# Attention and a state-space layer in one Trainium2 kernel: which score tiles go to VectorE, when a score fill is issued, and who goes first

## The chip, the cores and the metric

The kernel runs on one core of a Trainium2 chip. The core has five engines that matter here: TensorE (matrix products, "PE"), ScalarE (activation functions, "ACT"), VectorE ("DVE"), GpSimd ("POOL") and SyncE ("SP", which issues most DMA transfers). Each engine has its own in-order instruction stream and they meet through semaphores. Matrix products go to PSUM, which has eight banks of 512 float32 columns in each of 128 partitions. The metric is device time in microseconds; a comparison uses the median of several executions.

## What is computed

Two independent layers run on their own inputs, and their outputs are joined along the last axis.

```
# A: a diagonal complex state-space layer, L = 2048 steps, 640 states and channels
Lam_bar = exp(dt * Lam);  B_bar = ((Lam_bar - 1) / Lam)[:, None] * Bmat
h[t] = Lam_bar * h[t-1] + x[t] @ B_bar.T
y = 2 * Re(hseq @ Cmat.T) + x * Dskip
# B: attention, 2048 rows, 32 query heads of 20 channels, one key and one value head
q = x @ wq;  k = x @ wk;  v = x @ wv
p = softmax(q k^T * 20**-0.5)          # per head, no mask
out = concat_heads(p @ v) @ wo
```

The attention has 32 x 2048 x 2048 scores, each of which needs an exponential. That is by far the largest elementwise work of the kernel.

## The kernel before

**Tiles.** Heads are taken four at a time: eight head groups, for each of four blocks of 512 query rows. The code numbers these 32 blocks `b` (called head groups below). A block has 64 score tiles: 16 blocks of 128 keys times the four heads `j` of the group. A tile is 128 keys x 512 queries, fills one PSUM bank, and is one matmul of 32 contracted rows (20 channels, and one row that carries a bound for the softmax). Four tiles with four different `j` can run side by side in the array, since each uses its own 32 rows. There are 2048 tiles in all (`NTILE`).

**Two ways to an exponential.** Five banks belong to ScalarE: slot `SC0` of three banks and slot `SC1` of two. TensorE fills a slot (`fill`), ScalarE turns it into bf16 probabilities in one of seven buffers `PR` (L1040), and meanwhile the other slot is filled. About a fifth of the tiles go to VectorE instead: they are written to one of two other banks (`MB0`, `MB1`, which all other tasks share), and VectorE makes a first pass over the bank, an add and a clamp with int16 output whose bits are a coarse bf16 power (`fill_d`, into one of 18 buffers `DR`). Three shifted copies of that buffer (`copy`, by `copy_source` on VectorE or `pool_source` on GpSimd, one or two tiles at a time) make up the other terms of the approximation. So a VectorE tile has four entries in the product with V, a ScalarE tile one.

**PV.** The products with V accumulate a whole head group in the bank `MB2` (`pv_source`, `pv`). A group of four such matmuls, one for each head `j`, runs side by side in four column quarters. The `PR` or `DR` buffer that a matmul reads is free again when it is done. At the end of a head group VectorE evacuates the bank (`pvsb`, L1257) and the sums go through DRAM to be inverted and spread, so that the output can be normalized (`normalize`).

**Everything else** is cut into tasks with a due time in tiles, which `manager` starts when one of the two shared banks is free: projections of the queries, rows of the softmax bound, the state-space layer's input products (`unit_task`) and outputs (`y_task`), and the output projection (`o_task`). The state-space scans and their products run on VectorE.

**The order is planned when the program is built.** `Schedule` plays the engines with an assumed duration for each step (`dur`), and writes each engine's instructions in the order in which that play starts them. On the chip the order is fixed, and semaphores hold an engine until what it needs is there. An engine takes the ready step with the lowest `prio`. A step of `prio` at most `URGENT` (1.0) that will be ready soon holds back any step whose own `prio` is above 1.0 and which would run into it; steps at or below 1.0 are not held. A score fill has `prio` 0; `TASK`, `PV`, `ALONE` (a VectorE tile on its own) are TensorE's other priorities; `EV` (evacuations), `P1` (first pass), `COPY` and `COPY1` (copies), `CLOSE` (copies at the end of a group) are VectorE's. `port` marks steps of VectorE and GpSimd that must not overlap in the plan. `hurry` marks late state-space steps, which then get a priority of about 0.46, but only `PAUSE` ns after the last such step. `OVERDUE` is the number of tiles by which a task may be late before only the most urgent tasks are started.

**Which tile goes where.** Before, tiles are numbered in one sequence (`tile_n`). A fill takes the next three or two for ScalarE, and up to the fourth place of the array goes to VectorE if a shared bank and `DR` buffers are free (`want_d`) and VectorE's share stays below a quarter (`SHARE`); of the numbers taken, the one whose `j` has gone to VectorE least often is given to it (`d_weight`). The fill is issued as soon as its slot is free.

Of the kernel before, what the change touches and what calls it, by code (L numbers as in the profile page):

```python
# [9 lines left out]
ALU = mybir.AluOpType  # L10
# [10 lines left out]
class Op:  # L21


    __slots__ = ("eng", "fns", "dur", "deps", "prio", "reads", "writes", "prev", "gate", "hook", "start", "end",
                 "seq", "land", "dma_key", "idx", "tail", "mode", "load", "late", "port", "after")

    def __init__(self, eng, fns, dur, deps=(), prio=5, reads=(), writes=(), prev=None, gate=None, hook=None,
                 dma_key=None, land=0.0, tail=0.0, mode="F", load=0.0, port=False):
        self.eng, self.fns, self.dur = eng, list(fns), dur
        self.deps, self.prio, self.prev = list(deps), prio, prev  # L30
        self.reads, self.writes = list(reads), list(writes)
        self.gate, self.hook = gate, hook
        self.dma_key, self.land, self.tail = dma_key, land, tail
        self.mode, self.load, self.late = mode, load, False
        self.port, self.after = port, []
        self.start = self.end = None
        self.seq = self.idx = 0


class Schedule:  # L40
# [12 lines left out]

    PAUSE = 3300.0
    LOCK = 60.0
# [95 lines left out]
    def pick(self, eng):  # L151
        urgent = None
        t = self.t
        cands = self.pending[eng]
        for src in self.sources[eng]:
            extra = src()
            if extra is not None:
                cands = cands + [extra]
        can, held = [], []
        for op in cands:  # L160
            r = self.ready(op)
            if r is None:
                continue
            if op.gate is not None and not op.gate():
                continue
            if r <= t + 1e-6:
# [230 lines left out]
class Build:  # L397
# [189 lines left out]
    def program(self):  # L587
        self.tile_n = 0
        self.free_banks = list(self.banks)
        self.qt_op, self.row_op = {}, {}  # L590
# [388 lines left out]
    def attention(self):  # L979
# [10 lines left out]
        while self.tile_n < NTILE:  # L990
# [5 lines left out]
            n = min(self.CHUNKS[i], NTILE - self.tile_n)  # L996
            b0, b1 = self.tile_n // 64, min(self.tile_n + n, NTILE - 1) // 64
            yield lambda: self.block_ready(b0) and self.block_ready(b1)
            deps = list(self.slot_last[i])
            for b in sorted({b0, b1}):  # L1000
                deps += [self.row_op[self.row_key(b)]]
            deps += [self.kt_op[tb] for tb in range(4)]
            if k == 0:
                deps += self.tabs
            fill = self.pe([], self.mmt(512, 2), deps=deps, prio=0, mode="S", hook=lambda op, i=i: self.fill(op, i))
            k += 1

        for i in (k % 2, (k + 1) % 2):
            yield lambda: fill.start is not None and all(o.start is not None for o in self.slot_last[i])
            for bank in self.slots[i][1]:  # L1010
                bank.last, bank.busy = list(self.slot_last[i]), False
                self.misc.append(bank)
                self.free_banks.append(bank)

    def fill(self, op, i):
        p = self
# [3 lines left out]
        self.nhold += 1  # L1020
        tiles = list(range(self.tile_n, self.tile_n + n))
        self.tile_n += n
        extra = []
        while len(tiles) < 4 - len(extra) and self.want_d(len(extra)):
            tiles.append(self.tile_n)
            self.tile_n += 1
            extra.append(min(tiles, key=self.d_weight))
            tiles.remove(extra[-1])
            self.d_per[extra[-1] // 64, extra[-1] % 4] += 1
        ents = []  # L1030
# [3 lines left out]
        for m in extra:  # L1034
# [5 lines left out]
        ex = self.act(lambda e: e.activation(dst, t[:, 0:512 * n], ACT.Exp, scale=1.0 / UNIT),  # L1040
                      0.8333 * 512 * n + 50,
                      deps=[op], reads=[b.key for b in banks[:n]], writes=[f"PR{h.index}"], prio=0.5,
# [22 lines left out]

    def d_weight(self, m):

        return self.d_per[m // 64, m % 4], m

# [8 lines left out]
    def d_source(self):  # L1078

        if not self.started or not self.d_count or not self.want_d():  # L1080
            return None
        b = self.tile_n // 64
        if not self.block_ready(b) or self.d_per[b, self.tile_n % 4] > min(self.d_per[b, j] for j in range(4)):
            return None
        row = self.row_op[self.row_key(b)]
        if row.end is None or self.s.seen(row, "pe") > self.s.t:
            return None

        def hook(op):
            self.d_per[self.tile_n // 64, self.tile_n % 4] += 1  # L1090
            self.tile_n += 1
            self.fill_d(op, self.tile_n - 1)
            op.reads = sorted(set(op.reads))
        return Op("pe", [], self.mmt(512), prio=self.ALONE, mode="S", load=128.0, hook=hook)

    ALONE, TASK, PV = 1.9, 1.6, 2.0
    EV, P1, COPY, COPY1 = 0.52, 0.5, 0.49, 0.6
    CLOSE, PVEV = 0.3, 0.3
# [15 lines left out]
    def fill_d(self, op, m):  # L1114
# [9 lines left out]
        key = f"DR{h.index}"  # L1124
        first = self.dve(self.ts(p.DR[:, h.index, :], bank.ap, 16256.0, 0.0, ALU.add, ALU.max), 605, deps=[op],
                         reads=[bank.key], writes=[key], prio=self.P1)
# [13 lines left out]
    def copy_source(self):  # L1140
# [10 lines left out]
        k = can[0][2][0]  # L1151
        two = [d for d in can if k in d[2]][:2 if n >= 2 else 1]
        one = len(two) == 1
        if one and any(d[1].end is None or d not in can for d in self.d_open):
# [3 lines left out]
        if can[0][3] == self.pv_b and self.pv_filled[self.pv_b] == 64:  # L1158
            prio = self.CLOSE
        return Op("dve", [], 200 if one else 333, prio=prio, port=True, hook=lambda op: self.copy(op, k, two))  # L1160

    BACKLOG = 9

    def pool_source(self):
# [6 lines left out]
        two = [d for d in can if k in d[2]][:2]  # L1171
        if len(two) < 2:
            return None
# [543 lines left out]
    in_use = 0  # L1717
    OVERDUE = 120

# [75 lines left out]
```

## Time and profile before

| | us |
|---|---|
| median of 9 runs | 780.97 |
| lowest and highest | 779.97 and 782.89 |
| the profiled execution | 779.97 |
| its span in the profile | 777.9 |
| ScalarE busy | 757.5 |
| TensorE busy (matmul records) | 728.6 |
| VectorE busy | 656.8 |
| GpSimd busy | 379.7 |

The profile is one execution, recorded instruction by instruction. Busy time is the union of an engine's instructions. A line such as "L1040 ACT ACTIVATE PR<-SC ... x655 | 740.7, 1432 | 1.9 <-PE MB L569 1.5" is a group of equal instructions: the line of the code, engine, operation, what it writes and reads, how many there are, their busy time in us and the mean duration of one in ns, and then how long the engine was idle just before them and what released it. "MB" are the shared banks and the PV bank, "SC" the two slots of ScalarE. The chain of work is followed back from the last instruction: at each step to whatever released it. In its rows the first number is a start and the second a duration, both in us. TensorE's 32-row and 32-column matmuls are quarters of the array, so four of them lie beside each other in time.

### The profile page before, as it was taken

How to read it: one execution, taken by the hardware profiler on the slowest of the kernel's cores; microseconds unless marked ns; L12 is line 12 of the kernel's file. 1: busy time of each engine (PE TensorE's matmuls, PEld its weight loads, DVE VectorE, ACT ScalarE, POOL GpSimd, SP SyncE). 2: the span in 40 equal slices, each digit the busy share in tenths (PEclk: the TensorE clock that was granted, in tenths of full speed). 3: DMA queues.
4: the chain of work that ended last, by engine and by line, in shares of the span. 5: the costliest groups of instructions: out<-in, count | busy, mean ns of one | idle time of the engine just before them, and what ended most of it. 6: DMA issues, size and time to landing. Idle time of an engine off the chain costs nothing.

```text
span 777.9 us, 23546 instructions
## 1 busy us (share of the span) xinstructions
PE 728.6 (94%) x10148; PEld 236.5 (30%) x10150; DVE 656.8 (84%) x1249; ACT 757.5 (97%) x680; POOL 379.7 (49%) x395
## 2 busy tenths in 40 slices
PE   8999998899889999999998999999999999999898
PEld 3322222222223232223222323223222322333224
DVE  5988999999998978799998878788989878757994
ACT  5999999999999999999999999999999999999995
POOL 7044455555444112645546563464453565567552
PEclk9999999999999999999999999999999999999999
DMA  9830200000000000020000000010000010010001
GB/s 209 131 82 10 51 9 10 9 3 10 8 9 23 23 17 17 23 43 12 15 16 9 24 22 21 24 37 17 10 15 16 4 29 22 23 31 20 11 7 38
DMA packets 54183, 21.55 MB, mean 28 GB/s; under 512 B 43464, under 2 KB 54080, under 8 KB 54080
## 3 DMA queue, kind: packets, MB, share of 16 engines
q1 hardware_dynamic: 52072, 19.87, 11.4%
q8 instruction: 80, 1.31, 0.7%
q10 hardware_dynamic: 2008, 0.18, 0.2%
q14 instruction: 23, 0.19, 0.1%
HBM read 7.20 MB, written 5.50 MB: 16 GB/s over the span
## 4 chain that ended last, share of the span: by engine, by line
ACT 82%; PE 14%; DVE 2%; DMA 1%; issue 0%; ACTq 0%; DVEq 0%
ACT PR L1040 82%; PE MB L569 5%; PE SC L569 5%; PE MB L565 4%; DVE DR L584 1%; PE SC L565 1%; DMA vrow<-in_A_Dskip_dram 1%; DVE WO L716 0%; DVE xbT L793 0%; ACTq L550 0%; DVE fr L584 0%; DVE pvsb L1257 0%; DVE g L1553 0%; DVE wq L781 0%; DVE aq L583 0%
## 5 line engine op out<-in xcount | busy, mean ns | idle before, releaser
L1040 ACT ACTIVATE PR<-SC 128x1536 bf16<-128x1536 f32 (+1 forms) x655 | 740.7, 1432 | 1.9 <-PE MB L569 1.5
L579 POOL TENSOR_TENSOR DR<-DR,step 128x512 int32<-128x512 int32 x356 | 365.8, 1049 | 380.1 <-DVE DR L584 160.2
L584 DVE TENSOR_SCALAR DR<-MB 128x512 int16<-128x512 f32 x412 | 273.9, 683 | 75.1 <-PE MB L569 71.7
L569 PE MATMUL SC<-QT,KT 32*128 32x512 bf16 x1636 | 255.3, 383 | 38.7 <-ACT PR L1040 27.6
L569 PE MATMUL MB<-DR,VS 128*32 128x512 bf16 x1648 | 226.9, 384 | 2.6 <-DVE pvsb L1257 1.3
L569 PE MATMUL MB<-PR,VP 128*32 128x512 bf16 x1636 | 227.0, 385 | 1.0 <-DVE pvsb L1257 0.9
L569 PEld LDWEIGHTS SC<-QT,KT 32*128 32x128 bf16 x1636 | 66.2, 90 | 288.8 <-ACT PR L1040 220.5
L569 PE MATMUL MB<-QT,KT 32*128 32x512 bf16 x412 | 151.0, 384 | 0.7 <-DVE DR L584 0.6
L584 DVE TENSOR_SCALAR DR<-DR 128x1024 int16<-128x1024 int16 (+1 forms) x289 | 105.1, 416 | 4.0 <-PE MB L569 3.2
L569 PEld LDWEIGHTS MB<-PR,VP 128*32 128x32 bf16 x1636 | 56.8, 94 | 66.3 <-issue 48.5
L569 PEld LDWEIGHTS MB<-DR,VS 128*32 128x32 bf16 x1648 | 56.2, 94 | 66.0 <-issue 35.4
L565 PE MATMUL MB<-xaT,BT 128*32 128x512 bf16 x800 | 62.3, 382 | 0.0
L579 DVE TENSOR_TENSOR prod<-MB,Z 128x1024 bf16<-128x1024 f32 x40 | 48.6, 1215 | 6.8 <-PE MB L565 6.2
L569 PE MATMUL MB<-xbT,wqf 128*32 128x512 bf16 x640 | 47.8, 382 | 0.3 <-DVE brow L584 0.3
L565 PE MATMUL MB<-WO,OT 128*32 128x128 bf16 (+1 forms) x928 | 41.5, 292 | 0.0
L569 PEld LDWEIGHTS MB<-QT,KT 32*128 32x128 bf16 x412 | 35.4, 91 | 18.6 <-DVE DR L584 8.6
L1553 DVE TENSOR_TENSOR_SCAN g<-sc,hst,u 128x512 bf16<-128x512 f32 x30 | 38.9, 1299 | 0.0
L565 PE MATMUL MB<-CT,W 128*32 128x512 bf16 (+1 forms) x640 | 31.3, 301 | 0.0
L565 PE MATMUL MB<-CT,xbT 128*32 128x512 bf16 (+1 forms) x640 | 30.1, 301 | 0.0
L579 DVE TENSOR_TENSOR prod<-g,tab 128x1024 bf16<-128x1024 bf16 x40 | 29.3, 733 | 0.0
L1376 DVE CAST stg<-MB 128x512 bf16<-128x512 f32 x35 | 23.8, 681 | 6.3 <-PE MB L565 6.0
L569 PE MATMUL MB<-KT,VZ 128*32 128x256 bf16 x504 | 28.5, 275 | 0.0
(124 smaller groups left out, 377.1 us busy)
## 6 DMA issues: line engine op xcount, KB each, us to landing
out_dram<-stg SPq DMA_DIRECT2D x35, 128.0 KB, 1.7
rdB<-recs SPq DMA_DIRECT2D x124, 32.0 KB, 1.8
CT<-in_B_x_dram SPq DMA_DIRECT2D x2, 640.0 KB, 5.5
WO<-in_B_wo_dram SPq DMA_DIRECT2D x4, 200.0 KB
wqf<-in_B_wq_dram SPq DMA_DIRECT2D x1, 680.0 KB, 5.9
out_dram<-PR SPq DMA_DIRECT2D x5, 128.0 KB, 1.9
sums<-pvsb SPq DMA_DIRECT2D x31, 4.0 KB
dn<-sums SPq DMA_DIRECT2D x31, 4.0 KB, 1.9
```

The lines of the kernel that those rows point to most:

```text
L565: r = e.matmul(out[32 * j:32 * j + 32], lhsT=lhsT[:, 32 * j:32 * j + 32], rhs=rhs, start=start, stop=stop, tile_position=(0, 32 * j), skip ...
L569: return lambda e: e.matmul(out, lhsT=lhsT, rhs=rhs, start=start, stop=stop, **kw)
L579: return lambda e: e.tensor_tensor(out, a, b, op)
L584: return lambda e: e.tensor_scalar(out, a, s1, s2, op0=op0, op1=op1)
L1040: ex = self.act(lambda e: e.activation(dst, t[:, 0:512 * n], ACT.Exp, scale=1.0 / UNIT), 0.8333 * 512 * n + 50, deps=[op], reads=[b.key fo ...
L1376: ev = self.dve(lambda e: e.tensor_copy(st, bank.ap), 620, deps=[prev], reads=[bank.key], writes=[key], prio=self.EV, gate=(lambda: last.e ...
L1553: o = self.dve(lambda e, ri=ri, init=init: e.tensor_tensor_scan(p.g[:, u, ri, :], rdec, p.u[:, ri, :], init, ALU.mult, ALU.add), 1280, por ...
```

## The change

The list of tiles becomes, for each head group and head `j`, a queue of key blocks (`rem`). ScalarE takes its tiles from the head group at hand, and of it from the head with most tiles left (`take_tile`); VectorE takes tiles from that group while more than 10 tiles (`AHEAD`) are left in it, and else from the next group (`d_block`, `take_d`), if that group's queries are there and enough `DR` buffers remain for the copies that are still owed (`can_d`, `due_copies`). A copy takes one tile instead of two when the second belongs to a later group and buffers are short (`short`). A fill has a gate (`fill_now`): while the other slot's exponential runs, and no shared bank is free but one will be, the fill waits for the bank, at most until 650 ns (`MARGIN`) before that exponential ends, so that it can take a VectorE tile along. A gated fill counts as urgent from that moment (`due`). Copies come after first passes and evacuations (`COPY` 0.49 to 0.56), tasks of TensorE come before PV and are no longer held for a fill (`TASK` 1.6 to 0.95), `OVERDUE` goes from 120 to 400 and `PAUSE` from 3300 to 1000. The planner's assumed durations are changed for the exponential, the first pass and VectorE's copies.

```diff
-    PAUSE = 3300.0
+    PAUSE = 1000.0
@@ Schedule.pick
             if op.gate is not None and not op.gate():
+                if op.due is not None and r <= t + 1e-6 and (urgent is None or op.due < urgent):
+                    urgent = op.due
                 continue
@@ attention
-            b0, b1 = self.tile_n // 64, min(self.tile_n + n, NTILE - 1) // 64
-            yield lambda: self.block_ready(b0) and self.block_ready(b1)
+            near = [self.act_block()]
+            if self.remaining(near[0]) < n + 2 and near[0] + 1 < NQB * NGG:
+                near.append(near[0] + 1)
+            yield lambda: all(self.block_ready(b) for b in near)
...
             fill = self.pe([], self.mmt(512, 2), deps=deps, prio=0, mode="S", hook=lambda op, i=i: self.fill(op, i))
+            fill.gate = lambda op=fill, i=i, n=n: self.fill_now(op, i, n)
+    MARGIN = 650.0
+    def fill_now(self, op, i, n):
+        s = self.s
+        other = self.slot_last[1 - i]
+        if len(other) != 1 or other[0].start is None or not self.d_count:
+            return True
+        op.due = other[0].start + other[0].dur - self.MARGIN
+        if s.t >= op.due or not self.can_d() or len(self.d_free()) < len(self.SHIFTS):
+            return True
+        if len(self.d_banks()) >= self.WANT:
+            return True
+        for b in self.free_banks:
+            if all(o.end is not None for o in b.last):
+                r = max(s.seen(o, "pe") for o in b.last)
+                if s.t < r <= op.due:
+                    s.at(r)
+                    return False
+        return True
+    WANT = 1
@@ fill
-        tiles = list(range(self.tile_n, self.tile_n + n))
-        self.tile_n += n
-        extra = []
-        while len(tiles) < 4 - len(extra) and self.want_d(len(extra)):
-            tiles.append(self.tile_n)
-            self.tile_n += 1
-            extra.append(min(tiles, key=self.d_weight))
-            tiles.remove(extra[-1])
-            self.d_per[extra[-1] // 64, extra[-1] % 4] += 1
+        extra, used = [], set()
+        while len(extra) < 4 - n and self.want_d(len(extra)):
+            m = self.take_d(used)
+            if m is None:
+                break
+            extra.append(m)
+        tiles = [self.take_tile(used) for _ in range(n)]
...
-                      0.8333 * 512 * n + 50,
+                      0.8333 * 512 * n + 64,
+    def take_tile(self, used):
+        b = self.act_block()
+        for b, free in ((b, False), (b + 1, False), (b, True), (b + 1, True)):
+            can = [j for j in range(4) if b < NQB * NGG and self.rem[b][j] and (free or j not in used)]
+            if can:
+                return self.pop(b, min(can, key=lambda j: (-len(self.rem[b][j]), j)), used)
+    AHEAD = 10
+    def d_block(self):
+        b = self.act_block()
+        return b if self.remaining(b) > self.AHEAD else b + 1
+    def take_d(self, used):
+        if not self.can_d():
+            return None
+        b = self.d_block()
+        j = self.d_turn(b)
+        if j in used:
+            return None
+        self.d_per[b, j] += 1
+        return self.pop(b, j, used)
+    def can_d(self):
+        b = self.d_block()
+        if b >= NQB * NGG or not self.block_ready(b):
+            return False
+        row = self.row_op[self.row_key(b)]
+        if row.end is None or self.s.seen(row, "pe") > self.s.t:
+            return False
+        if b > self.pv_b and len(self.d_free()) < len(self.SHIFTS) + self.due_copies():
+            return False
+        return bool(self.rem[b][self.d_turn(b)])
+    def d_turn(self, b):
+        return min(range(4), key=lambda j: (self.d_per[b, j], -len(self.rem[b][j]), j))
+    def due_copies(self):
+        return sum(len(d[2]) for d in self.d_open if d[3] <= self.pv_b)
...
-    ALONE, TASK, PV = 1.9, 1.6, 2.0
-    EV, P1, COPY, COPY1 = 0.52, 0.5, 0.49, 0.6
+    ALONE, TASK, PV = 1.9, 0.95, 2.0
+    EV, P1, COPY, COPY1 = 0.52, 0.5, 0.56, 0.6
@@ fill_d: the first pass is planned with 663 instead of 605 ns
@@ copy_source
+        if self.short(two):
+            two = two[:1]
...
-        return Op("dve", [], 200 if one else 333, prio=prio, port=True, hook=lambda op: self.copy(op, k, two))
+        return Op("dve", [], 210 if one else 342, prio=prio, port=True, hook=lambda op: self.copy(op, k, two))
+    def short(self, two):
+        return len(two) > 1 and two[1][3] > self.pv_b and len(self.d_free()) < 1 + self.due_copies()
@@ pool_source
-        if len(two) < 2:
+        if len(two) < 2 or self.short(two):
@@ manager
-    OVERDUE = 120
+    OVERDUE = 400
```

## The prediction

> **What bounds the kernel now.** First the page: engine shares, then the chain that ended last.
>
> ```profile
> PE 728.6 (94%) x10148; PEld 236.5 (30%) x10150; DVE 656.8 (84%) x1249; ACT 757.5 (97%) x680; POOL 379.7 (49%) x395
> ...
> PEclk9999999999999999999999999999999999999999
> ...
> ACT 82%; PE 14%; DVE 2%; DMA 1%; issue 0%; ACTq 0%; DVEq 0%
> ...
> L1040 ACT ACTIVATE PR<-SC 128x1536 bf16<-128x1536 f32 (+1 forms) x655 | 740.7, 1432 | 1.9 <-PE MB L569 1.5
> ```
>
> The 655 exponentials of L1040 carry 82% of the chain, and ScalarE was idle only 1.9 us before them. TensorE's 94% says less: its matmuls overlap. The groups with their forms split the exponentials:
>
> ```profile
> L1040 ACT ACTIVATE PR<-SC 128x1536 bf16<-128x1536 f32 x327 | 537.9, 1645 | 1.9 <-PE MB L569 1.5 <-PE SC L569 0.3
> L1040 ACT ACTIVATE PR<-SC 128x1024 bf16<-128x1024 f32 x327 | 399.1, 1221 | 0.1
> ```
>
> Their means overlap (537.9 + 399.1 is more than the stage), so I price them by pitch, from the chain in order of time:
>
> ```profile
> 24.38 47.67 ACT PR L1040 x42
> ...
> 82.74 2.19 DVE WO L716
> ...
> 339.21 131.22 ACT PR L1040 x116
> ...
> 559.91 1.70 DVE DR L584 x4
> 561.60 0.60 DVE prod L579
> 562.20 1.35 DVE DR L584 x4
> ...
> 571.77 193.56 ACT PR L1040 x171
> ```
>
> 116 exponentials in 131.22 us and 171 in 193.56 us give 2.262 and 2.264 us for a pair (1536 + 1024 columns). 327 pairs are 739.7 us, the odd 512-column one about 0.48 (a third of 1536's share). The first starts at 24.38, the last ends at 766.72 (ScalarE's timeline: 738.78 + 27.94): 742.3 us. So some 2.2 us are lost there: a change of this stage can win by fewer exponentials, and hardly by fewer waits. Between those stretches the chain runs through TensorE. Its timeline shows how near it is:
>
> ```profile
> 541.57 0.39 PE L569 MATMUL SC<-QT,KT 32*128 32x512 bf16 x3
> 541.58 0.39 PE L569 MATMUL MB<-QT,KT 32*128 32x512 bf16 x1
> 541.89 0.40 PE L569 MATMUL MB<-PR,VP 128*32 128x512 bf16 x4
> 542.12 0.39 PE L569 MATMUL MB<-xbT,wqf 128*32 128x512 bf16 x4
> 542.44 0.39 PE L569 MATMUL SC<-QT,KT 32*128 32x512 bf16 x2
> 542.75 1.05 PE L569 MATMUL MB<-xbT,wqf 128*32 128x512 bf16 x16
> 543.74 0.39 PE L569 MATMUL SC<-QT,KT 32*128 32x512 bf16 x3
> ```
>
> From fill to fill it took 0.87 us with 8 quarter matmuls between (two groups of four side by side) and 1.30 us with 16: 0.215 us for a group, 0.44 for a fill with both switches (VectorE's extra tile, "MB<-QT,KT", runs beside the fill's own). A pair of fills with six groups costs 0.88 + 6 x 0.215 = 2.17 us, with seven 2.39. ScalarE's pair is 2.262. So six groups fit and seven don't, unless an earlier pair left slack. Last, who makes ScalarE wait:
>
> ```profile
> ACT PR L1040 <- PE MB L569: 1.5, 5, 0.3
> ...
> ACT PR L1040 <- PE SC L569: 0.3, 1, 0.3
> ```
>
> "PE MB" is the PV matmul that frees a PR buffer, so the order of TensorE's stream, not lack of score tiles, causes most of its few waits.
>
> **The change, part by part.** I counted in the two built instruction lists.
>
> *Fewer exponentials.* 327 + 327 + 1 become 325 + 325: 11 score tiles more go by VectorE (412 to 423). Two pairs and the odd one: 2 x 2.262 + 0.48 = 5.0 us less on the path. This term is a count times a pitch; I hold it to 0.1 us.
>
> *VectorE and GpSimd.* First passes +11 x 0.683 = +7.5 us; two-tile copies -30 x 0.445 = -13.4; one-tile copies -37 x 0.292 = -10.8: VectorE 656.8 - 16.7 = 640 us. GpSimd takes 65 more two-tile copies x 1.049 = +68 us, 448 in all. Both fit in the stage; what covers GpSimd's is its 398 us of idle. Off the path as totals; if the cover were gone, PV groups would wait a copy's 1.05 us.
>
> *TensorE.* PV matmuls +33 (two lists: DR +44, PR -11), 8 groups x 0.215 = 1.8 us; keep-warm matmuls +292 = 73 groups of 256 columns x 0.11 = 7.9 us; score tiles stay 2048. They fill gaps, but not all: TASK 1.6 to 0.95 puts projections, scan inputs and output matmuls above PV and frees them from the planner's hold before an urgent fill, OVERDUE 400 lets overdue tasks pile up, and a fill may now stand later. In disjoint pairs of fills, those with seven or more groups (keep-warm counted by its columns) are 3 of 327 before and 50 of 324 after. Bounds: nothing, if slack absorbs all; 47 x (2.39 - 2.26) = 6.1 us and about 1 more for the eight- and nine-group ones, if none is. To choose, I went down both lists with these prices, letting a fill start when the exponential of its slot ended and an exponential when its fill and the last PV on its PR buffer were through. Before: 6 late exponentials, 1.05 us; the two large ones (0.44, 0.39) fall at the exponentials that the trace shows waiting at 260.44 and 288.01 (0.34 idle each). After: 16, together 3.5 us, the worst 1.1. So +2.5 us, nearer the lower end because 4- and 5-group pairs stand around the heavy ones.
>
> *Fills that wait for a bank (fill_now).* Behind a held fill stand PV and task matmuls, which the planner runs first; the waiter is ScalarE's next exponential. Fills with an extra tile that wait for VectorE: 273 in 655 before, 288 in 650 after; those whose bank was last used in the fill just before, 71 to 111. There VectorE's first pass (0.683) must end between two fills, about 1.1 us apart on average. What the trace lost to VectorE is 2.2 less 1.05, some 1.2 us, for instance behind the 2.19 us memset and the run of copies quoted. Scaled by 111/71 it is 1.9: +0.7 us. Bounds: -1.2 (all such losses go, since the planner's first pass is now 663 ns, near the 683 measured, and copies now yield to first passes) and +14 (0.34 us, the trace's typical wait, at each of 40 new tight places). I take +0.7, as the trace hid most such waits: fills waited 38.8 us for VectorE in 77 cases and ScalarE almost nothing.
>
> *Tiles of the next head group.* With 10 tiles or fewer left in a group, VectorE starts the next one's. That removes the bunching of copies at a group's end (GpSimd idle until VectorE: 160.2 us) and costs DR buffers held longer. No instruction of its own; bounds -1.0 us (the two waits near the group ends at 260 and 288 plus one like them) to +1.0 us (the same number of PV waits for a buffer); I take 0, as the walk above already contains its order.
>
> *Queues.* SP's list has 338 instructions in both, GpSimd issues no DMA, and the DMA engines are busy 12% of the span. The row and output transfers move earlier or later by single steps; cover: the queue's idle time. Bounds 0 to 2 us (one late row transfer, 1.8 us to land); I take 0.
>
> *Head and tail.* Up to the first exponential the streams agree but for two small VectorE steps off the path: 0. At the end, before, TensorE reached the last PV 0.7 us after the last exponential; after, the last fill precedes 2.26 us of exponentials instead of 1.4, so that PV is ready about 0.5 us sooner; but 76 instead of 60 output matmuls follow the last normalization (+16 / 4 x 0.215 = +0.86), and 0.3 us may come back from output groups moved past the last evacuation. Bounds -0.5 to +0.9; I take 0.
>
> [...]
>
> **Sum:** -5.0 + 2.5 + 0.7 + 0 = -1.8 against the profiled execution (779.97 us, span 777.9, 2.1 outside it): span 776.1, execution 778.2. That execution lies 1.0 below the median of the runs, 780.97; taken from the median, 779.2 us. A measurement of this kernel can tell about 0.2% (1.6 us), so my value lies just beyond that line, 779.4.
>
> **Rivals.**
> 1. *The extra load is absorbed* (chance 0.15). Only the 5.0 us show: 776.0. For it: the fills' slack; against: 50 seven-group pairs, and the walk's 1.1 us place.
> 2. *It comes out even* (0.25). TensorE's order returns 4 us instead of 2.5 and VectorE 1: 781. For it: I price switches at their best; the chain's own pieces (0.37 for a fill, 0.98 for 16) sum 0.05 higher per fill. Against: the walk on the old list shows no such extra losses.
> 3. *TensorE becomes the bound of the middle* (0.15), slower. If most of the 50 heavy pairs follow one another without slack, they cost up to 7 us, and with 10 pairs of six pushed over by later fills at 0.34 us, 3.4 more: -5.0 + 7 + 3.4 = +5.4, some 786. Decides from 37 unabsorbed heavy pairs (37 x 0.135 = 5.0). Against: only 16 late places in the walk.
> 4. *The change does not do what it says*: excluded as to counts, since the built list holds 650 exponentials.
>
> My own case holds 0.45, spread 777.5 to 780.5, two thirds of it below 779.4. Faster: 0.15 + 0.30 = 0.45, and a little of case 2, 0.48. Same: the rest of mine, most of 2 and the near part of 3: 0.36. Slower 0.16. The range takes in 1 and the near half of 3: 775.9 to 784.0; my case alone 777.5 to 780.5.
>
> **What the changed profile would show.** 325 + 325 exponentials at an unchanged pitch of 2.26 us a pair; ScalarE's stage from 24.4 to about 764.7; idle before L1040 4 to 5 us instead of 1.9, most of it until "PE MB"; a wait of about 1 us near two thirds of the span; GpSimd near 448 us, VectorE 640. I am wrong if ScalarE's waits are mostly for VectorE's first passes ("PE SC" behind "DVE DR"), if the idle is under 2.5 or above 7 us, or if the tail after the last exponential moves from 11.2 us by over 1.

## The result and the profile after

The changed kernel takes 786.51 us (median of 10 runs, 784.76 to 788.73), the kernel before 781.12 in the runs made beside it. The ratio is 1.007, with an interval of 1.006 to 1.0079: slower by 0.7%, where 779.2 was predicted and 784.0 was the end of the range. The profiled execution took 785.61 (span 783.9; before 779.97 and 777.9).

First the page of the changed kernel: engine shares, TensorE's granted clock, chain, and the group of the exponentials.

```profile
PE 733.7 (94%) x10473; PEld 245.1 (31%) x10475; DVE 654.7 (84%) x1193; ACT 754.4 (96%) x675; POOL 444.8 (57%) x460
...
PEclk9989999999999999999999999999999999999999
...
ACT 64%; PE 26%; DVE 5%; DMA 2%; SPq 1%; issue 1%; POOL 0%; ACTq 0%; DVEq 0%; POOLq 0%
...
L1068 ACT ACTIVATE PR<-SC 128x1536 bf16<-128x1536 f32 (+1 forms) x650 | 737.5, 1338 | 10.8 <-PE MB L571 6.7
```

There are 650 exponentials instead of 655, as counted, but ScalarE stood idle 10.8 us before them instead of 1.9. The chain now goes through TensorE for 26% of the span instead of 14%, and one digit of the clock, the third, around 50 us, is an 8: new.

The first exponential starts at 24.39 us and the last ends at 772.34: 748.0 us, against 742.3 before. 325 pairs at the old pitch of 2.262 us are 735.2, so 12.8 us are lost in the stage instead of 2.2. That is the bill: -5.0 for five exponentials, +10.6 for new losses, +0.3 for the tail (11.2 to 11.5 us), together 5.9 of the 6.0 us by which the span grew. The idle time gives 8.9 of the 10.6. The rest is about 1.7; I put it down to the same places (21 waits, 6 before), since an exponential that starts after a pause has no predecessor to overlap with. The sizes fit: a pair that stands alone takes 2.37 us (rows below) where the pitch is 2.262, and 15 more such places at 0.11 are 1.6 us (an estimate).

The stages show where. The windows view of the changed kernel has for each stretch its length, then busy us of PE, PEld, DVE, ACT and POOL with their instructions, the granted clock, the DMA share and GB/s:

```profile
core 0: us, PE busy (x) PEld busy (x) DVE busy (x) ACT busy (x) POOL busy (x), PEclk, DMA share, GB/s
40.00:60.00 20.00, 17.07 (x206) 4.90 (x198) 15.22 (x28) 16.47 (x15) 10.34 (x11) 0.83 0.43 70
450.00:500.00 50.00, 48.70 (x611) 15.02 (x607) 38.46 (x67) 48.48 (x44) 30.12 (x30) 0.97 0.05 16
500.00:550.00 50.00, 45.99 (x738) 15.91 (x738) 42.75 (x76) 47.85 (x43) 25.55 (x26) 1.00 0.13 26
```

Before, ScalarE (the fourth pair of numbers) was busy 20.00 of 20, 49.87 of 50 and 49.71 of 50 us there; the first of these rows in the kernel before:

```profile
40.00:60.00 20.00, 18.66 (x221) 5.27 (x217) 17.01 (x34) 20.00 (x19) 10.29 (x10) 1.00 0.36 75
```

So 3.5 us go between 40 and 60 us, where nothing was lost, and 3.7 instead of 0.4 between 450 and 550. In the first stretch ScalarE's timeline (start, length, what, and in brackets the idle time before it and its releaser) reads:

```profile
39.88 6.97 ACT L1068 ACTIVATE PR<-SC 128x1024 bf16<-128x1024 f32 x6
48.43 1.02 ACT L1068 ACTIVATE PR<-SC 128x1024 bf16<-128x1024 f32 x1 [1.58 <-PE SC L571]
49.65 2.37 ACT L1068 ACTIVATE PR<-SC 128x1536 bf16<-128x1536 f32 x2 [0.20 <-PE MB L571]
52.88 2.37 ACT L1068 ACTIVATE PR<-SC 128x1536 bf16<-128x1536 f32 x2 [0.86 <-PE MB L571]
56.13 2.37 ACT L1068 ACTIVATE PR<-SC 128x1536 bf16<-128x1536 f32 x2 [0.88 <-PE MB L571]
```

One wait for a fill, and then a pair of exponentials about every 3.2 us instead of every 2.26. The timeline of the other engines a little earlier:

```profile
43.19 2.97 SPq L964 DMA_DIRECT2D QT<-brow  x4
...
44.73 0.39 PE L571 MATMUL SC<-QT,KT 32*128 32x512 bf16 x3
44.74 0.38 PE L571 MATMUL MB<-QT,KT 32*128 32x512 bf16 x1
...
47.37 0.37 PE L571 MATMUL MB<-QT,KT 32*128 32x512 bf16 x1 [2.24 <-DMA QT<-brow]
...
48.00 0.39 PE L571 MATMUL SC<-QT,KT 32*128 32x512 bf16 x2
```

The instruction that waits 2.24 us is a VectorE tile ("MB<-QT,KT") of the next head group. It needs the row that carries that group's softmax bound, which `row_task` copies from `brow` into QT by four DMAs on SP (`row_op`). VectorE wrote the row at 33.26 to 33.85 us, but SP began to issue its transfer at 43.19. In TensorE's stream the fill that ScalarE needs stood behind that early tile; it started at 48.00 us. SP's timeline says why the transfer came late:

```profile
21.50 7.54 SPq L556 DMA_TRANSPOSE BT<-in_A_B_re_dram  x5
29.09 6.52 SPq L556 DMA_TRANSPOSE BT<-in_A_B_im_dram  x5
35.66 7.49 SPq L556 DMA_TRANSPOSE CT<-in_A_C_re_dram  x5
43.19 2.97 SPq L964 DMA_DIRECT2D QT<-brow  x4
```

SP issues without a break. In the three groups ahead of the row a transpose takes it 1.30 to 1.51 us on average where the planner has 1.30 (`loadT`), each of these row DMAs 0.74 where it has 0.57 (`dma`); on the chip the row lands at 47.23. In the kernel before SP's list is the same up to there. Three rows of its timelines, SP's and TensorE's:

```profile
43.50 2.98 SPq L960 DMA_DIRECT2D QT<-brow  x4
...
48.19 0.40 PE L569 MATMUL MB<-KT,VZ 128*32 128x256 bf16 x8
48.62 0.40 PE L569 MATMUL SC<-QT,KT 32*128 32x512 bf16 x3
```

TensorE waited for nothing there, because its first instruction that needs the row is the fill at 48.62 us (experiment 4 shows that it is this one). The change did not delay the transfer; it moved the first need of it ahead by some 3.5 us (from 48.62 to 45.13, where the wait begins), to before it lands.

Then the clock. Windows of the changed kernel over the same place, columns as above:

```profile
44.00:46.00 2.00, 1.11 (x15) 0.26 (x12) 1.93 (x4) 2.00 (x3) 1.37 (x3) 1.00 0.11 23
46.00:48.00 2.00, 0.64 (x6) 0.20 (x7) 0.44 (x2) 0.84 (x1) 2.00 (x3) 1.00 0.18 43
48.00:50.00 2.00, 2.00 (x31) 0.62 (x27) 1.18 (x3) 1.38 (x2) 0.72 (x1) 0.80 1.51 115
50.00:52.00 2.00, 2.00 (x26) 0.53 (x19) 1.35 (x4) 2.00 (x2) 0.00 (x0) 0.50 0.23 45
52.00:54.00 2.00, 2.00 (x19) 0.40 (x14) 2.00 (x5) 1.14 (x2) 0.68 (x1) 0.50 0.64 136
54.00:56.00 2.00, 2.00 (x26) 0.73 (x24) 0.44 (x1) 1.24 (x2) 1.40 (x2) 0.50 0.39 82
56.00:58.00 2.00, 1.85 (x23) 0.43 (x19) 1.87 (x4) 1.87 (x2) 0.84 (x1) 0.99 0.00 0
```

TensorE was busy 1.11 and then 0.64 of 2 us, and from 49.2 to 56.0 us it was granted half its clock, while it was busy all the time. The 6.83 us are two periods of 3.41: the other stretch in this profile's stage, 452.0 to 455.4, is 3.41 us long, and one of experiment 3 lasts 10.2. The 3.4 us ahead of 49.2 were not idle, TensorE was busy 1.83 of 3.40 us in them; at what load a period starts is not shown.

### The profile page after: what moved, and what is told of

Its sections match the earlier page's. It is cut to its first block, busy times and chain, and to the rows that moved or that the text cites. A ratio compares the mean times of both kernels' runs of the same rounds, so it can differ in the third digit from the quotient of the medians.

```text
span 783.9 us, 24235 instructions
## 1 busy us (share of the span) xinstructions
PE 733.7 (94%) x10473; PEld 245.1 (31%) x10475; DVE 654.7 (84%) x1193; ACT 754.4 (96%) x675; POOL 444.8 (57%) x460
## 4 chain that ended last, share of the span: by engine, by line
ACT 64%; PE 26%; DVE 5%; DMA 2%; SPq 1%; issue 1%; POOL 0%; ACTq 0%; DVEq 0%; POOLq 0%
ACT PR L1068 64%; PE MB L571 10%; PE MB L567 8%; PE SC L571 7%; DVE DR L586 1%; DMA recs<-rc 1%; PE SC L567 1%; DVE QT L918 1%; SPq L556 1%; DMA vrow<-in_A_Dskip_dram 1%; DMA rdB<-recs 0%; DMA xaT<-in_A_x_dram 0%; DVE VS L585 0%; DVE xbT L797 0%; DVE WO L720 0%
## 5 line engine op out<-in xcount | busy, mean ns | idle before, releaser
L1068 ACT ACTIVATE PR<-SC 128x1536 bf16<-128x1536 f32 (+1 forms) x650 | 737.5, 1338 | 10.8 <-PE MB L571 6.7
L581 POOL TENSOR_TENSOR DR<-DR,step 128x512 int32<-128x512 int32 x421 | 430.8, 1046 | 317.2 <-DVE DR L586 114.8
L586 DVE TENSOR_SCALAR DR<-MB 128x512 int16<-128x512 f32 x423 | 282.6, 684 | 81.1 <-PE MB L571 76.9
L571 PE MATMUL MB<-QT,KT 32*128 32x512 bf16 x423 | 154.2, 386 | 3.2 <-DMA QT<-brow 2.2
L586 DVE TENSOR_SCALAR DR<-DR 128x1024 int16<-128x1024 int16 (+1 forms) x222 | 83.6, 426 | 8.3 <-PE MB L571 6.0
L567 PE MATMUL MB<-xaT,BT 128*32 128x512 bf16 x800 | 57.8, 382 | 0.5 <-DMA xaT<-in_A_x_dram 0.3
L571 PEld LDWEIGHTS MB<-QT,KT 32*128 32x128 bf16 x423 | 36.2, 91 | 22.7 <-issue 10.8
L571 PE MATMUL MB<-KT,VZ 128*32 128x256 bf16 x796 | 43.0, 283 | 0.0
L1633 DVE TENSOR_TENSOR_SCAN g<-sc,hst,u 128x512 bf16<-128x512 f32 x30 | 40.7, 1363 | 0.0
L581 DVE TENSOR_TENSOR prod<-g,tab 128x1024 bf16<-128x1024 bf16 x40 | 32.7, 818 | 0.0
L567 PE MATMUL MB<-CT,W 128*32 128x512 bf16 (+1 forms) x640 | 29.4, 300 | 0.7 <-issue 0.7
```

Of the source, the lines that this page charges most:

```text
L567: r = e.matmul(out[32 * j:32 * j + 32], lhsT=lhsT[:, 32 * j:32 * j + 32], rhs=rhs, start=start, stop=stop, tile_position=(0, 32 * j), skip ...
L571: return lambda e: e.matmul(out, lhsT=lhsT, rhs=rhs, start=start, stop=stop, **kw)
L581: return lambda e: e.tensor_tensor(out, a, b, op)
L586: return lambda e: e.tensor_scalar(out, a, s1, s2, op0=op0, op1=op1)
L1633: o = self.dve(lambda e, ri=ri, init=init: e.tensor_tensor_scan(p.g[:, u, ri, :], rdec, p.u[:, ri, :], init, ALU.mult, ALU.add), 1280, por ...
```

## The experiments

Two theories were set against each other. Theory A: the row transfer stands too late in SP's list for the early tile, and TensorE's wait and the half clock after it make the loss. Theory B: TensorE's new order makes it, with projections and other tasks ahead of PV (`TASK`) and heavy pairs of fills one after another, which is the prediction's third rival. Line numbers shift by four where four lines are added. Except where "order only" is said, an edit lets the planner play the whole kernel again, so everything after it can move; such a run prices a version, not one instruction. "Order only" means that one queue's finished list is changed and nothing else. Every ratio is to the kernel before, in runs beside it.

**1. The row first (order only, changed kernel).** The row's four DMAs go ahead of the transposes of the first half of CT.

```diff
                 self.s.run()
+                order = self.s.order
+                late = self.ct_op[0]
+                order.remove(late)
+                order.insert(order.index(self.row_op[(0, 0)]) + 1, late)
```

> The changed kernel with one transfer order altered: on SP the five transposes of CT (real part) come after the first row transfer instead of before it; every instruction of the other engines stays in its place. In the changed kernel's profile TensorE stands 2.24 us before a VectorE tile of the second head group until this row transfer lands (47.37 us), its granted clock is then 0.5 from 49.2 to 56.0 us, and ScalarE loses about 4.0 us between 43 and 56 us. Theory A (a transfer that comes too late for the early tile, and the clock that falls because of the wait): the row lands some 7 us earlier, the 2.24 us wait and the half clock go, 786.5 - 4.0 = 782.5 us, ratio to the kernel before about 1.002. Theory B (TensorE's order alone makes the kernel slower, the early waits would be made up for): 786, less than 1 us better, with the loss reappearing in the next 50 us.

Measured: 781.63 us (12 runs), ratio 1.001 [1.0001, 1.0018]. The edit gives back 4.9 us of the loss, and ScalarE is busy 20.00 of 20 us between 40 and 60. SP's timeline of this kernel, and ScalarE's group from its page:

```profile
35.76 3.31 SPq L968 DMA_DIRECT2D QT<-brow  x4
39.11 6.56 SPq L560 DMA_TRANSPOSE CT<-in_A_C_re_dram  x5
```

```profile
L1072 ACT ACTIVATE PR<-SC 128x1536 bf16<-128x1536 f32 (+1 forms) x650 | 737.4, 1334 | 7.8 <-PE MB L575 6.1
```

This settles what most of the extra loss is: instructions of TensorE, ScalarE, VectorE and GpSimd are the same, in the same order, and four DMAs on another queue are worth 4.9 us. It leaves the kernel even with the one before, not ahead of it: of 7.8 us of idle, 6.1 are still "PE MB". (The profiled execution, 783.13, was the longest of the twelve.)

**2. Tasks held again.** Theory B's suspect alone, without the row.

```diff
-    ALONE, TASK, PV = 1.9, 0.95, 2.0
+    ALONE, TASK, PV = 1.9, 1.6, 2.0
```

> The changed kernel with the priority of tasks on TensorE back at 1.6 (held before urgent fills, as before). The planned order changes throughout; 651 exponentials, 421 VectorE tiles. Theory A: the first row transfer is still wanted early, so most of the loss around 45 to 56 us stays, and only part of the 4.1 us that ScalarE loses at places where TensorE's order has too much between fills goes: 785 us. Theory B: the order of tasks is the cause: 782 us or less, with ScalarE's wait for PV matmuls (6.7 us in the changed kernel) down to about 2 us.

Measured: 782.3 us, but from 779.27 to 786.15 in 10 runs; ratio 1.0017 [1.0, 1.0034]. The expectations do not separate here (785, or 782 with ScalarE's waits for "PE MB" down to about 2 us; they are 4.3), and the trace says why: in the new plan the first need of the row came later.

```profile
PE SC L571 <- DMA QT<-brow: 1.1, 1, 1.1
```

That is TensorE's wait in this kernel: 1.1 us instead of 2.2. In the profiled execution (780.39) the clock stayed at 1.000 throughout. Over its runs the mean granted clock went from 1.000 to 0.989 and the time from 779.8 (mean of the two at 1.000) to 786.2. So one program, with a wait of about half the length, met no half-clock periods in some runs and, by the mean, five in another (0.011 of 781 us is 8.6 us of clock lost; at half rate that takes 17.2 us, five periods of 3.41): 6.3 us for five, some 1.3 us each. That is an estimate from one run at 0.989.

**3. Fills never wait for a bank.**

```diff
-        if len(other) != 1 or other[0].start is None or not self.d_count:
+        if True or len(other) != 1 or other[0].start is None or not self.d_count:
```

> The changed kernel with fill_now always true: a fill never waits for a bank. 654 exponentials, 414 VectorE tiles, so 3.8 exponentials' time (about 4.4 us) more on ScalarE than in the changed kernel; the early use of the row transfer stays. Theory A: the waiting fills cost little by themselves, so it is slower by up to the 4.4 us: 787 to 791 us. Theory C (fills that wait to the last moment make ScalarE late behind VectorE's first passes): the losses outside the first 60 us, about 8 us in the changed kernel, fall by more than 4.4 us, and it is faster than the changed kernel: 784 us or less.

Measured: 788.76 us, ratio 1.0097 [1.0079, 1.0115], with 654 exponentials. That is 2.2 us more than the changed kernel, where four more exponentials are 4.5 us by themselves. So the waiting of fills is not the cause of the loss: without it ScalarE is still idle for 10.2 us before its exponentials (10.8 with it). TensorE waits 2.8 us for the same row, and the half clock lasts from 49.7 to 59.9 us, three periods.

**4. The row late in the kernel before (order only).** If theory A holds, the old kernel must lose the same way when its row is late.

```diff
+                order = self.s.order
+                late = self.row_op[(0, 0)]
+                order.remove(late)
+                order.insert(order.index(self.ct_op[1]) + 1, late)
```

> The kernel before with one transfer moved: the first row transfer after both groups of CT transposes on SP, all else in its place. The transfer then lands some 6.5 us later, near 54 us; the first score fill of the second head group needs it at about 47.5. Theory A (a late row transfer stops TensorE, and an idle TensorE then runs at half clock for some us): 5.5 us of wait and 1.3 to 3 us for one or two windows at half clock, 788 to 790 us, the granted clock in the rows from 50 to 60 us well below 1. If the clock has no part: 786 to 787 us. If other work hides the transfer: 781 us.

Measured: 788.27 us, ratio 1.0099 [1.0083, 1.0114]. Two rows of TensorE's timeline and one of ScalarE's waits in this kernel:

```profile
48.54 0.40 PE L573 MATMUL MB<-KT,VZ 128*32 128x256 bf16 x8
55.67 0.61 PE L573 MATMUL SC<-QT,KT 32*128 32x512 bf16 x3 [6.73 <-DMA QT<-brow]
```

```profile
ACT PR L1044 <- PE MB L573: 8.5, 6, 6.6
```

The fills ahead of the eight matmuls at 48.54 run although the row is not there; the first that needs it is the one after them, which begins to wait at 48.94. In the kernel before that fill stands at 48.62, and not near 47.5 as I had expected here and in the next run. The clock was halved from 52.4 to 59.2 us, half of that inside the wait. The old kernel, with none of the change in it, gets slower by 7.4 us when four DMAs move behind the second half of CT's transposes.

**5. The row first in the kernel before (order only).** The control: the edit of experiment 1 there.

> The kernel before with the first row transfer ahead of the CT transposes on SP, all else in its place: the control for the first experiment. Theory A: in the kernel before nothing waited for this transfer (its first user starts near 47.4 us, when it has just landed), so the edit is worth nothing there: 780.9 us, within 0.1% of the kernel before. If the transposes' place itself were worth time whoever needs the row (by less transfer traffic at some moment), it would win 1 us or more here too.

Measured: 780.79 us against 780.75, ratio 0.9999 [0.9985, 1.0014]. The edit gives nothing where nothing waits for the row, so its 4.9 us in experiment 1 are no general gain of a better list.

**6. The row first, and tasks held.** Experiment 1 with `TASK` 1.6.

> The changed kernel with the first row transfer ahead of the CT transposes and TASK at 1.6. 651 exponentials, 421 VectorE tiles; places with too much between fills 3.9 us together, as many as with 0.95 (3.5). With the transfer late and TASK 1.6 it took 782.3 us with a granted clock between 0.989 and 1. Theory A (the transfer and the clock, not the task priority): 780 to 781 us, at most 1.5 us from the 781.6 of TASK 0.95, and the clock at 0.998 or 1. Theory B (the priority is a cause by itself): 778.5 us or less.

Measured: 780.41 us, ratio 0.999 [0.9977, 1.0003], 651 exponentials, "PE MB" 4.7 us in 8 waits. Once the row is early, `TASK` moves the median by 1.2 us only. That tests the priority; the heavy pairs of fills stay, since by the walk down the list this kernel has 3.9 us of them and experiment 1 has 3.5. What rules out theory B as the main cause is experiment 1, where TensorE's order is untouched. As a smaller cause it stays.

**7. All next-group tiles away.** Experiment 1 with VectorE kept in the group at hand.

```diff
-    AHEAD = 10
+    AHEAD = 0
```

> The changed kernel with the first row transfer ahead of the CT transposes and AHEAD 0, so that VectorE never takes tiles of the next head group. 644 exponentials, 438 VectorE tiles. 6 fewer exponentials are 6.8 us less on ScalarE than in the first experiment (781.6), but the copies bunch at the end of each group and TensorE's order has 14 us of too much between fills, 10.6 more. If the tiles of the next group are what lets VectorE's share grow without PV waits: 784 to 787 us. If they are of no use: 778 us or less.

Measured: 794.53 us, ratio 1.0173 [1.0158, 1.0188], more than expected. ScalarE's waits in this kernel:

```profile
ACT PR L1072 <- PE MB L575: 23.1, 12, 12.1
```

The longest, 12.1 us near 220 us, stands in the chain as a row of VectorE's scans, products and copies from 204.7 to 224.0. The tiles of the next group, which I priced at nothing, are worth 13 us to this version of the plan (794.53 - 781.63), although this kernel has six exponentials less. I take the reason to be that with them VectorE's work at the end of a group is spread out; the rows of the chain fit that, and no run shows it by itself.

**8. The row first, and the old pause.** `PAUSE` spaces the late state-space steps that VectorE does first.

```diff
-    PAUSE = 1000.0
+    PAUSE = 3300.0
```

> The changed kernel with the first row transfer ahead of the CT transposes and PAUSE back at 3300 (late state-space steps take precedence on VectorE less often). 647 exponentials, 432 VectorE tiles. In the first experiment the transfer alone gave 781.6 us with 650. Theory A (once the early wait for the transfer is gone, the number of exponentials and the TensorE-heavy places set the time): 3 exponentials fewer are 3.4 us, the places about the same (4.2 against 3.5 us by the order), so 779 us. Theory D (a shorter PAUSE was what kept VectorE's tiles in time; without it the waits behind first passes and output tasks grow): 783 us or more.

Measured: **776.89 us** (775.83 to 777.38), ratio 0.995 [0.9936, 0.9965], faster than both kernels. The page of this kernel:

```profile
L1072 ACT ACTIVATE PR<-SC 128x1536 bf16<-128x1536 f32 (+1 forms) x647 | 732.9, 1353 | 6.6 <-PE MB L575 5.1
```

Three exponentials less than experiment 1 (3 x 1.13 = 3.4 us) and 1.2 us less idle, of a gain of 4.7. That is bookkeeping; why the shorter pause costs three exponentials was not tried by itself.

**9. The row first, a margin for it, and the old place of copies.** The planner lets VectorE take a next-group tile only 3 us after the row is seen, and copies go back ahead of first passes and evacuations.

```diff
-        if row.end is None or self.s.seen(row, "pe") > self.s.t:
+        if row.end is None or self.s.seen(row, "pe") + 3000.0 > self.s.t:
-    EV, P1, COPY, COPY1 = 0.52, 0.5, 0.56, 0.6
+    EV, P1, COPY, COPY1 = 0.52, 0.5, 0.49, 0.6
```

> The changed kernel with the first row transfer ahead of the CT transposes, VectorE's tiles of a head group not before 3000 ns after its row is planned to be there, and copies ahead of first passes again (COPY 0.49). 650 exponentials, as in the changed kernel; the order of TensorE's list has too much between fills at 15 places, 1.7 us together instead of 3.5. Theory A: 781.6 less 1.9, some 779.5 us, and TensorE at half clock in fewer windows. Theory D (copies ahead of first passes make the banks late, and ScalarE waits behind VectorE): 783 us or more, ScalarE's idle until a score fill over 5 us.

Measured: 777.33 us, ratio 0.9958 [0.9941, 0.9975]. It has 650 exponentials, as many as the changed kernel, and this idle time:

```profile
L1072 ACT ACTIVATE PR<-SC 128x1536 bf16<-128x1536 f32 (+2 forms) x650 | 736.6, 1346 | 3.5 <-PE MB L575 2.0
```

This run supports the first term of the prediction: with five exponentials less and 1.6 us more idle than in the kernel before, it is 3.6 us faster (777.33 against 780.88). It also prices what experiment 1 still lost: same count, 4.3 us less in the medians, and in the profiles 4.3 us less idle (experiment 1's profile being of its longest run). Which of the two edits brought that, the margin or the place of the copies, no run separates.

**10. Old pause, fills never waiting.** Experiment 8 with the edit of experiment 3.

> The fifth experiment's kernel (first row transfer first, PAUSE 3300; 776.9 us) with fill_now always true, so that no fill waits for a bank. 651 exponentials against 647, 422 VectorE tiles against 432; too much between fills 5.1 us against 4.2. Theory A (the waiting fills bring VectorE tiles and cost little): 4 exponentials and 0.9 us more, 782 us. Theory C (the waiting fills cost as much as they bring): 777 us or less.

Measured: 784.4 us, ratio 1.0047 [1.003, 1.0064]. Without waiting fills the best version loses 7.5 us: four exponentials more, 2.2 us more idle, and half-clock stretches at 51.4 to about 54.8 and 89.0 to 95.8 us. So in this version `fill_now` is one of the parts that pay.

**11. Row first, margin, old pause.** Copies stay as the change has them.

```diff
-    PAUSE = 1000.0
+    PAUSE = 3300.0
-        if row.end is None or self.s.seen(row, "pe") > self.s.t:
+        if row.end is None or self.s.seen(row, "pe") + 3000.0 > self.s.t:
```

> The changed kernel with three edits: the first row transfer ahead of the CT transposes as in the first experiment, VectorE's tiles of a head group not before 3000 ns after its row transfer is planned to be there, and PAUSE back at 3300. 643 exponentials and 442 VectorE tiles: 7 fewer exponentials than the changed kernel (about 8 us), 12 fewer than the kernel before (13.6 us). Theory A: without the transfer wait and the half clock, the fewer exponentials show: 786.5 - 4.0 - 8 + 2 (more TensorE-heavy places) = 776 to 778 us, faster than the kernel before. Theory B (TensorE bounds): 783 us or more in spite of the fewer exponentials.

Measured: 789.93 us, ratio 1.0126 [1.0104, 1.0148], a clear miss. There are only 643 exponentials, the last ends at 762.0, 10 us before the changed kernel's, and then ScalarE waited:

```profile
778.48 0.60 ACT L1458 ACTIVATE PR<-MB 128x512 bf16<-128x512 f32 x1 [16.49 <-PE MB L571]
```

The tail was 24.7 us long. One row of TensorE's timeline there, of several like it:

```profile
766.42 2.33 PE L571 MATMUL SC<-CT,xbT 128*32 128x512 bf16 x40
```

TensorE had matmuls of the state-space outputs left when the last exponential ended ("CT,xbT" and "diagD,xaT", `y_task`; they make up most of the chain until 777.8, and then come 96 of the output projection): more due tasks had piled up than went between the fills. The changed kernel has none of these state-space matmuls in its tail. That `OVERDUE` 400 allows the pile is read from the code; no run changed it alone.

**12. Four edits.** Row first, old pause, old place of copies, the row's margin, and `MARGIN` 750 instead of 650.

> The changed kernel with the first row transfer first, PAUSE 3300, COPY 0.49, the 3000 ns margin for VectorE tiles after a row transfer, and MARGIN 750: a trial for a better version. 648 exponentials, 429 VectorE tiles, 3.1 us of too much between fills (4.2 in the fifth experiment). Theory A: one exponential more and 1.1 us less of it, 776 to 777.5 us, like the fifth and sixth. If COPY and MARGIN act through VectorE's waits: 780 us or more, with ScalarE's idle until a score fill up.

Measured: 778.13 us (776.62 to 779.26), ratio 0.9963 [0.995, 0.9977]: no better than experiment 8, with 648 exponentials, 5.8 us idle and a mean granted clock of 0.991 in most runs. What is good in two versions of the plan does not add up in a third.

## Why the prediction was wrong

**Queues: the step that failed.** It costed SP's list at nothing, with bounds of 0 to 2 us and "the queue's idle time" as cover. The bound named the right event, a late row transfer. But the cover was not there: SP issues without a break from before 21.5 up to 54 us, and the row's transfer sat ready for 9.3 us (33.85 to 43.19). The DMA engines' 12% share, which I quoted, did not show it: even from 40 to 60 us, with SP issuing until 54.1, it is 43%. The price was wrong too, since I took the transfer's own 1.8 us; the wait cost 2.24 us of TensorE, and then two half-clock periods: together 4.9 us (experiment 1). The split was not tried; at the 1.2 to 1.3 us a period that runs of the kernel before and of experiment 2 give, it would be 2.24 + 2.5 (an estimate).

**Tiles of the next head group: where the new need came from.** I gave them "no instruction of its own" and looked for waits for DR buffers only. Their input, the row, was not checked, although `can_d` asks for it in the diff. The planner asks by its own durations, and these were short by 0.2 us for many of SP's transposes and by 0.17 for each row DMA.

**TensorE's order: right in kind, too small in the sum.** Late places were foreseen: 16 waits for "PE MB" (5 before) are in the changed kernel, as many as the walk had, though by luck, since three of them stand in the half clock at 50 us; and so is the 1 us wait near two thirds of the span that I named (1.05 us before the exponential at 507). Here are ScalarE's waits after, in us, times, longest:

```profile
ACT PR L1068 <- PE MB L571: 6.7, 16, 1.0
...
ACT PR L1068 <- PE SC L571: 3.7, 5, 1.6
```

Of the 6.7 us, 1.9 belong to the half clock at 50 us. The other 4.8 stand against 1.5 before: +3.3, where I had +2.5. What I left out altogether is the lost overlap, the 1.7 us above. In the medians, experiment 1, which has no late row, is 0.55 us above the kernel before: so everything but the row ate 5.5 us where I had allowed 3.2 for the order and VectorE. That is 2.3 us of the miss; the queue is the other 4.9. How the 2.3 divide between the order and VectorE no run shows.

**VectorE.** Predicted +0.7, bounds -1.2 to +14. The trace shows one place of size, at 454 to 456 us: between 448 and 452 us a fill waited 0.40 us for its slot and a VectorE tile on its own 0.25 for a first pass, TensorE was busy 1.60 of 2 us in each of the two windows, and a single half-clock period (452.0 to 455.4) followed; ScalarE lost 1.17 us. That the lighter load brought the half clock is not shown: TensorE was busy 2.63 us in the 3.42 ahead of it, but also only 2.48 of 3.41 from 288.07 to 291.48, and there the clock stayed at 1.00. Experiment 1 passes the same place with ScalarE busy 49.52 instead of 48.48 of 50 us.

VectorE's total was 655 us, where I had 640 (GpSimd's 445, where I had 448). First passes rose by 8.7 us and copies fell by 21.5, near the working. But other steps became longer. Two groups of VectorE after, which had means of 458 and 449 ns before, and one step three times, with the GpSimd copies around it, from the timelines:

```profile
L581 DVE TENSOR_TENSOR W<-prod 128x512 bf16<-128x512 bf16 x20 | 11.7, 583 | 0.0
L581 DVE TENSOR_TENSOR xbT<-prod 128x512 bf16<-128x512 bf16 x20 | 11.2, 559 | 0.1
```

```profile
300.17 1.43 POOL L581 TENSOR_TENSOR DR<-DR,step 128x512 int32<-128x512 int32 x1 [0.22 <-PE MB L571]
300.29 0.40 DVE L581 TENSOR_TENSOR xbT<-prod 128x512 bf16<-128x512 bf16 x1
...
327.62 2.03 POOL L581 TENSOR_TENSOR DR<-DR,step 128x512 int32<-128x512 int32 x2 [2.67 <-DVE prod L581]
329.10 0.83 DVE L581 TENSOR_TENSOR xbT<-prod 128x512 bf16<-128x512 bf16 x1
...
332.14 0.41 DVE L581 TENSOR_TENSOR xbT<-prod 128x512 bf16<-128x512 bf16 x1
```

The same step takes 0.41 us at 332.14, with no GpSimd copy beside it, and 0.83 where GpSimd's copies ran until 329.65, 0.55 us into it: 0.42 us longer, where standing still for all of the 0.55 would give 0.96. At 300.29 it is not longer, and there the GpSimd copy beside it takes 1.43 us, where the median of these copies is 1.04. Why the step is longer in the one place and the copy in the other, no run shows. VectorE's measured total is 15 us above my working, and VectorE remained 84% busy. No run tells what of it reached ScalarE.

**Fewer exponentials, head and tail: right.** 650, and the pitch is unchanged: the last 17 pairs, without a wait, take 38.71 us in ScalarE's timeline, 2.277 a pair with the last one's full length in it. The tail moved by 0.3 us.

**The rivals.** Rival 3 gave 786, and 786.5 was measured, but by a mechanism that it did not name: the heavy pairs can have cost at most 2.3 us more than I had allowed, as experiment 1 shows, so the match of the number was luck. The chance of 0.16 for slower was priced on TensorE's load alone. By my own list I was to be wrong if the idle went above 7 us, and it is 10.8. Without the late row the case would have been my rival 2, even.

**What stays open.** Why the shorter pause costs 4.7 us in the plan with the row first; whether the margin or the place of the copies makes experiment 9 fast; what starts the remaining half-clock periods, whose number differs between runs of one program; and how far each edit's price holds outside the plan that it was tried in.

## What to carry to other kernels

When a change lets an engine start on later work sooner, list what that work reads and find in the trace when each piece lands, down to the queue that issues it; a queue that is full of long issues has no idle time to hide anything, whatever the DMA engines' share says (here SP issued without a break from 21.5 to 54.1 us, at a share of 12% over the span). Price a wait of TensorE by the wait and by what the clock does afterwards (here 2.24 us, and then 6.83 at half clock). And when a plan's parts are judged, change a finished order in one place as well as replanning: only the first says what one instruction costs.

## What the hardware showed that I had not expected

- A wait of 2.24 us in TensorE's stream, in a kernel where TensorE is busy 94%, was followed by 6.83 us at half clock, one of 2.8 us by 10.2. One of 6.73 us had 6.8, of which 3.3 lay inside the wait. A wait of 1.1 us was followed by none in the profiled execution.
- The price is uneven. In the kernel before, 32 runs at a mean granted clock of 1.000 average 780.1 us and seven at 0.996 average 782.3 (1.8 periods of 3.41 us: some 1.2 us each). In experiment 12 a run at 0.996 took 776.62 and one at 0.989 779.02 (3.2 periods: 0.75 us each), and in experiment 8 the one run at 0.998 took the mean of the three at 1.000, 776.75. These are single runs, but a period's price does not look fixed; what TensorE has to do in it may be the reason, and was not tried.
- The mean duration of an exponential record fell from 1645 to 1551 ns for 1536 columns, with an unchanged pitch of the pairs. One that stands alone takes 1.45 us (1.02 for 1024 columns, and a pair 2.37, not 2.47), and the records together are longer than the stage (504.2 + 365.7 us in 748.0), so they overlap where one exponential is queued behind another; where ScalarE has to wait there is less of that, and the mean looks better.
